# fp32 weight pieces on the SyncE queue, and a few transposes moved between DMA and TensorE, in a fused BigBird attention and gMLP kernel

## The chip, the cores and the metric

The kernel runs on one core of one Trainium2 chip. The metric is the time of one execution in device microseconds, as the median of several runs. Beside the runs there is one profiled execution. Its span goes from the first to the last instruction of the program; its own time is a little longer than the span.

## The reference

What is computed is block-sparse attention followed by a gMLP layer with a spatial gate:

```python
scores = scale * np.matmul(q, k.transpose(0, 1, 3, 2))       # (4, 8, 768, 768), scale = 1/8
# mask: blocks of 32; neighbours, first and last block, 3 sampled blocks per block
scores = np.where(mask, scores, -1000000000.0)
attn = softmax(scores)                                       # with 1e-09 in the sum
x = np.matmul(attn, v)                                       # to (4, 768, 8 * 64)

h = np.maximum(x @ w_in, 0.0)                                # w_in (512, 1024)
u, v = h[..., :512], h[..., 512:]
v_n = (v - mean(v)) / np.sqrt(var(v) + 1e-06)
v_s = np.einsum('ts,bsd->btd', w_spatial, v_n) + b_spatial[None, :, None]   # w_spatial (768, 768)
out = (u * v_s) @ w_out                                      # w_out (512, 512), fp32 out
```

All inputs but the sampled blocks are fp32. The batch is 4, with 8 heads of 64 and a sequence of 768.

## The kernel before

The work is cut into 16 pairs of heads (4 pairs to a batch), and each pair into 12 slots, so that the main loop is an order written out by hand: for each slot of each pair it issues the scores of one 128-row chunk of keys, one exp of 128x768 on ScalarE (line 260), the product with v of the chunk seven slots back (`av`, line 272), and whatever else is hung on that slot. Every engine runs its own instructions in this program order. The tile framework inserts the waits on semaphores.

The life of a pair p is this. `load` (line 95) brings q, k, v as fp32 on the SyncE queue, three pairs ahead, in slot 7 of pair p-3 (pairs 0 to 2 at the start). The staging tiles `st_q`, `st_k`, `st_v` have two buffers each. `prepare` (lines 109 and 112) casts them on Pool in slot 7 of pair p-2, k first, then q, then v; v goes to one of three `vv` buffers. Then q and k have to be transposed. For pairs 1 to 4 this is done on TensorE in thirds (`tr_pair`, lines 206 and 211: two transposes in each of six slots, then copies from PSUM by VectorE), in slots 4 to 9 of pair p-1 (6 to 11 for pair 1). For later pairs it is done by a DMA transpose on the SyncE queue (`tr_dma`, line 239) in slot 10 of pair p-2, and VectorE copies the halves in slots 5 and 9 of pair p-1 (`split_pair`, line 245).

After the last `av` of a head VectorE normalises it (`norm`, lines 285 and 286), in slots 0 and 6. The normalised pair is transposed to `xt` in slot 8 of the next pair (`xtr`): by a DMA transpose on the SyncE queue (line 299), or, for the last pair of a batch, by six transposes on TensorE and one copy (lines 295 and 297).

The gMLP of batch 0 begins after slot 8 of pair 4. Its 24 units (six each of v, u, spatial and out; lines 348, 371, 393, 411) are spread over the 48 slots that follow by a budget of TensorE time. The same happens for batches 1 and 2; the last batch is run at the end, alone. The gMLP's buffers `un`, `vsb`, `vn`, `gn`, `gt` have two copies each of 6 KB per partition and stand empty until pair 4.

The weights come by three DMAs on Pool's queue, which cast fp32 to bf16 on the way: w_spatial in slot 0 of pair 0 (line 463), w_in and w_out in slot 7 of pairs 0 and 1 (lines 470 and 473). w_spatial is transposed on TensorE, 36 blocks with six copies, in slots 0 to 3, 10 and 11 of pairs 2 and 3 (`wspt_third`, lines 312 and 317).

Three things about waits matter below. A load waits until the cast on Pool has freed its buffer. The SyncE queue issues in program order[...]. PSUM has two buffers for scores, two for `av` and two (`moe`) for transposes and gMLP units.

Of the kernel before, what the change touches and what calls it, by code (L numbers as in the profile page):

```python
# [10 lines left out]
FP32 = mybir.dt.float32  # L11
BF16 = mybir.dt.bfloat16
# [14 lines left out]
def kernel(  # L27
# [16 lines left out]
    nc = tc.nc  # L44

    B, H, S, D = q.shape
# [3 lines left out]
    NCH = S // 128  # L50
# [3 lines left out]
    DH = DFF // 2  # L54
    NDM = DM // 128
    NDH = DH // 128
    NG = H // 2
    NP = B * NG
# [5 lines left out]
    work = ctx.enter_context(tc.tile_pool(name="work", bufs=1))  # L64
    psum = ctx.enter_context(tc.tile_pool(name="psum", bufs=1, space=bass.MemoryType.PSUM))
    ctx.enter_context(tc.manual_schedule())

    ident = const.tile([128, 128], BF16)
    warm = const.tile([128, 512], BF16)
    w_in_t = const.tile([128, NDM, DFF], BF16)  # L70
    w_out_t = const.tile([128, NDH, DM], BF16)
    ws_nat = const.tile([128, NCH, S], BF16)
    w_spt = const.tile([128, NCH, S], BF16)
# [10 lines left out]
    def dram(src, b, h0, nh):  # L84
        return src[b, h0:h0 + nh].rearrange("h (p c) d -> p h (c d)", c=NCH)

    def st_tile(p, nm):
        st[nm, p] = work.tile([128, 2, NCH * D], FP32, tag=f"st_{nm}", bufs=2, name=f"st_{nm}")
        return st[nm, p]

    def load(p, names="qkv", eng=nc.sync):
        b, g = divmod(p, NG)
        for nm, src in (("q", q), ("k", k), ("v", v)):
            if nm in names:
                eng.dma_start(out=st_tile(p, nm), in_=dram(src, b, 2 * g, 2))
# [3 lines left out]
    def nat_tile(p, nm):  # L99
        nat[nm, p] = work.tile([128, NCH, 2, D], BF16, tag=f"nat_{nm}", bufs=2,  # L100
                               name=f"nat_{nm}")

    def cast_qk(p, nm, hs, eng):
        src = st[nm, p][:, hs].rearrange("p h (c d) -> p h c d", d=D)
        dst = nat[nm, p].rearrange("p c h d -> p h c d")[:, hs]
        if eng is nc.scalar:
            nc.scalar.activation(out=dst, in_=src, func=AF.Copy)
        else:
            eng.tensor_copy(out=dst, in_=src)  # L109

    def cast_v(p):
        nc.gpsimd.tensor_copy(  # L112
            out=vv[p % 3][:, :, :, 0:D],
            in_=st.pop(("v", p)).rearrange("p h (c d) -> p h c d", d=D))

    def prepare(p):
        for nm in "kq":
            nat_tile(p, nm)
            cast_qk(p, nm, slice(0, 2), nc.gpsimd)
        cast_v(p)  # L120

    samp_i = const.tile([NB, 2 * NR], I32)
    stq, stk = st_tile(0, "q"), st_tile(0, "k")
# [21 lines left out]
    def keep_warm(n, cols):  # L145
        for _ in range(n):
            nc.tensor.matmul(out=wps[:, 0:cols], lhsT=warm[:, 0:128], rhs=warm[:, 0:cols],  # L147
                             start=True, stop=True)
# [50 lines left out]
    tr_ps = {}  # L199
# [30 lines left out]
    def second_head():  # L230
        mask_rows(1)
        cast_qk(0, "k", slice(1, 2), nc.vector)
        cast_qk(0, "q", slice(1, 2), nc.vector)
# [15 lines left out]
    a_ref, av_ref, xn_ref, xt_ref = {}, {}, {}, {}  # L249

    def qk_exp(j, ci):
        if ci == 0:
            a_ref[j] = work.tile([128, NCH, S], BF16, tag="a_all", bufs=3, name="a_all")
        ps = psum.tile([128, 1024], FP32, tag="sc", bufs=2)
        for hf in range(2):
            nc.tensor.matmul(out=ps[:, hf * 512:hf * 512 + HALF],  # L256
                             lhsT=kt[j % 4][:, ci * 128:(ci + 1) * 128],
                             rhs=qt[j % 4][:, hf * HALF:(hf + 1) * HALF],
                             start=True, stop=True)
        nc.scalar.activation(  # L260
            out=a_ref[j][:, ci, :].rearrange("p (b c) -> p b c", b=2),
            in_=ps.rearrange("p (b c) -> p b c", b=2)[:, :, 0:HALF],
            func=AF.Exp, scale=0.125)
# [15 lines left out]
    def norm(j):  # L279
        p, h = divmod(j, 2)  # L280
        if h == 0:
# [4 lines left out]
        nc.vector.tensor_tensor(out=xn_ref[p][:, :, h, :], in0=ps[:, :, 0:D],  # L286
                                in1=rc.to_broadcast([128, NCH, D]), op=ALU.mult)

    def xtr(p):
        xn = xn_ref.pop(p)  # L290
        xt_ref[p] = work.tile([128, S], BF16, tag="xt", bufs=8, name="xt")
        if p % NG == NG - 1:
            ps = psum.tile([128, S], BF16, tag="moe", bufs=2)
            for c in range(NCH):
                nc.tensor.transpose(out=ps[:, c * 128:(c + 1) * 128], in_=xn[:, c],
                                    identity=ident)
            nc.vector.tensor_copy(out=xt_ref[p], in_=ps)
        else:
            nc.sync.dma_start_transpose(
                out=xt_ref[p].rearrange("p (c n) -> p c n", c=NCH),  # L300
                in_=xn.rearrange("p c h d -> p (c h d)"))


    ws_ps = {}

    def wspt_third(i):
        sc, third = divmod(i, 3)
        if third == 0:
            ws_ps[0] = psum.tile([128, S], BF16, tag="moe", bufs=2, name="ps_ws")
        ps = ws_ps[0]  # L310
        for tcc in (2 * third, 2 * third + 1):
            nc.tensor.transpose(
                out=ps[:, tcc * 128:(tcc + 1) * 128],
                in_=ws_nat[:, tcc, :].rearrange("p (s c) -> p c s", c=NCH)[:, sc, :],
                identity=ident)
        if third == 2:
            nc.vector.tensor_copy(out=w_spt[:, sc, :], in_=ps)

    tail_tags = deque(["sc", "av", "moe"])

# [109 lines left out]
    for p in range(NP + 1):  # L430
        for s in range(12):
            g = 12 * p + s
            j, ci = divmod(g, NCH)
            if p == NP and g - LAG >= 2 * NP * NCH:
                break
            if p < NP:
                qk_exp(j, ci)
            if p == 0 and s == 0:
                second_head()
            if p == 0 and s < 6:  # L440
                keep_warm(2, 128)
            if p == 0 and s == 3:
                tr_head(1, "k", dve_copy)
            if p == 0 and s == 4:
                tr_head(1, "q", dve_copy)
                mask_rows(2)
                mask_rows(3)
            if p + 1 <= NG:
                first = 4 if p else 6
                if first <= s < first + 3:  # L450
                    tr_pair(p + 1, "k", s - first)
                elif first + 3 <= s < first + 6:
                    tr_pair(p + 1, "q", s - first - 3)
            elif p + 1 < NP and s in (5, 9):
                split_pair(p + 1, "k" if s == 5 else "q")
            if s == 10 and NG < p + 2 < NP:
                tr_dma(p + 2, "k")
                tr_dma(p + 2, "q")
            if p == 0 and s == 0:
                cast_v(0)  # L460
                prepare(1)
                load(2)
                nc.gpsimd.dma_start(out=ws_nat,
                                    in_=moe_w_spatial.rearrange("(p c) s -> p c s", c=NCH))
            if s == 7 and p + 2 < NP:
                if p + 3 < NP:
                    load(p + 3)
                prepare(p + 2)
                if p == 0:
                    nc.gpsimd.dma_start(out=w_in_t,  # L470
                                        in_=moe_w_in.rearrange("(g p) f -> p g f", p=128))
                if p == 1:
                    nc.gpsimd.dma_start(out=w_out_t,
                                        in_=moe_w_out.rearrange("(g p) f -> p g f", p=128))
            if moe_q and slots_left > 0:
                budget += sum(u[0] for u in moe_q) / slots_left
                slots_left -= 1
                while moe_q and budget >= moe_q[0][0] / 2:
                    ns, run = moe_q.popleft()
                    run()  # L480
                    budget -= ns
            if g >= LAG:
                ja, qc = divmod(g - LAG, NCH)
                av(ja, qc)
                if qc == NCH - 1:
                    norm(ja)
            if p in (2, 3) and not 4 <= s < 10:
                for i in range(3 * (s if s < 4 else s - 6) // 2, 3 * (s + 1 if s < 4 else s - 5) // 2):
                    wspt_third(9 * (p - 2) + i)
            if s == 8 and p >= 1:  # L490
                xtr(p - 1)
                if p % NG == 0:
                    moe_q.extend(moe_units(p // NG - 1))
                    slots_left = 48
                    budget = 0.0
# [35 lines left out]
```

## Time and profile before

| what | value |
|---|---|
| median of 7 runs | 232.79 us (231.63 to 235.83) |
| profiled execution, its own time | 233.34 us |
| its span | 231.6 us |
| TensorE matmul busy | 216.5 us, 93% of the span |
| ScalarE busy | 171.3 us, 74% |
| VectorE busy | 132.2 us, 57% |
| Pool busy | 51.5 us, 22% |
| DMA moved | 37.32 MB, mean 161 GB/s |
| mean granted TensorE clock | 0.985 |

Busy time is the union of the instructions of an engine. Matmuls are pipelined and their ends are modelled, so that a TensorE shown as busy is not at its peak. PEld is the loading of weights into TensorE's array and overlaps the matmuls. The DMA figure counts written bytes. A wait is put down to the instruction or transfer that ended it last.

### The profile page before, as it was taken

How to read it: one execution, taken by the hardware profiler on the slowest of the kernel's cores; microseconds unless marked ns; L12 is line 12 of the kernel's file. 1: busy time of each engine (PE TensorE's matmuls, PEld its weight loads, DVE VectorE, ACT ScalarE, POOL GpSimd, SP SyncE). 2: the span in 40 equal slices, each digit the busy share in tenths (PEclk: the TensorE clock that was granted, in tenths of full speed). 3: DMA queues.
4: the chain of work that ended last, by engine and by line, in shares of the span. 5: the costliest groups of instructions: out<-in, count | busy, mean ns of one | idle time of the engine just before them, and what ended most of it. 6: DMA issues, size and time to landing. Idle time of an engine off the chain costs nothing.

```text
span 231.6 us, 5286 instructions
## 1 busy us (share of the span) xinstructions
PE 216.5 (93%) x2125; PEld 131.9 (57%) x2154; DVE 132.2 (57%) x285; ACT 171.3 (74%) x245; POOL 51.5 (22%) x82
## 2 busy tenths in 40 slices
PE   7899999939999999999999999999999999999993
PEld 3567787625556555566566555666565555544551
DVE  6683575315799334347996444359992333576432
ACT  5899999943689866796799667887799676257241
POOL 5332650440126401020153401210160000012000
PEclk9999999995999999999999999999999999999999
DMA  6579999999309584799928372999240323520015
GB/s 214 194 222 215 367 182 180 330 225 331 105 0 108 201 116 81 231 228 301 336 44 200 109 136 49 268 284 282 43 96 9 76 52 63 198 94 0 0 48 228
DMA packets 54941, 37.32 MB, mean 161 GB/s; under 512 B 38404, under 2 KB 51204, under 8 KB 54788
## 3 DMA queue, kind: packets, MB, share of 16 engines
q1 hardware_dynamic: 53428, 33.83, 57.3%
q0 software_dynamic: 1200, 2.75, 7.0%
q8 instruction: 17, 0.28, 0.5%
q10 hardware_dynamic: 288, 0.39, 0.5%
q14 instruction: 8, 0.07, 0.1%
HBM read 24.38 MB, written 6.29 MB: 132 GB/s over the span
## 4 chain that ended last, share of the span: by engine, by line
PE 81%; DMA 6%; ACT 6%; DVE 2%; issue 2%; SPq 1%; POOL 0%; POOLq 0%
PE ps L256 25%; PE ps_av L272 12%; PE ps_moe L393 10%; PE ps_moe L348 7%; PE ps_moe L371 7%; ACT a_all L260 6%; PE ps_moe L411 6%; DMA st_k<-in_k_dram 5%; PE ps_t L393 2%; PE wps L147 2%; PE ps_t L348 2%; PE ps_t L411 1%; PE ps_t L371 1%; PE ps_sc L393 1%; DMA out_dram<-osb 1%
## 5 line engine op out<-in xcount | busy, mean ns | idle before, releaser
L260 ACT ACTIVATE a_all<-ps 128x768 bf16<-128x768 f32 x192 | 143.2, 811 | 36.8 <-PE ps L256 36.5
L256 PE MATMUL ps<-qt,kt 88*128 88x384 bf16 x384 | 94.6, 327 | 4.4 <-ACT a_all L260 3.2
L272 PEld LDWEIGHTS <-a_all 128*128 128x128 bf16 x1152 | 61.0, 98 | 30.0 <-issue 1.2
L272 PE MATMUL ps_av<-vv,a_all 128*128 128x65 bf16 x1152 | 68.0, 194 | 0.0
L256 PEld LDWEIGHTS <-kt 88*128 88x128 bf16 x384 | 28.9, 98 | 8.2 <-issue 5.2
L396 DVE SCALAR_TENSOR_TENSOR gn<-ps_moe,b_col,un 128x512 bf16<-128x512 f32 x18 | 13.5, 751 | 28.2 <-PE ps_moe L393 28.2
L393 PE MATMUL ps_moe<-vn,w_spt 128*128 128x512 bf16 x99 | 24.8, 378 | 0.5
L112 POOL CAST vv<-st_v 128x768 bf16<-128x768 f32 x16 | 13.6, 851 | 47.6 <-PE ps_av L272 39.3
L393 PEld LDWEIGHTS <-w_spt 128*128 128x128 bf16 x144 | 13.8, 97 | 14.3
L348 PE MATMUL ps_moe<-w_in_t,xt 128*128 128x512 bf16 x66 | 19.5, 401 | 0.5 <-DMA st_k<-in_k_dram 0.2
L109 POOL CAST nat_k<-st_k 128x768 bf16<-128x768 f32 x15 | 12.5, 835 | 32.4 <-DMA st_k<-in_k_dram 20.9
L361 POOL TENSOR_SCALAR std<-mv 128x3 f32<-128x3 f32 x8 | 1.9, 243 | 78.0 <-DVE mv L358 65.8
L286 DVE TENSOR_TENSOR xn<-ps_av,rc 128x384 bf16<-128x384 f32 x32 | 17.8, 558 | 1.4 <-DVE rc L285 0.3
L411 PE MATMUL ps_moe<-w_out_t,gt 128*128 128x512 bf16 x66 | 18.1, 378 | 0.3
L371 PE MATMUL ps_moe<-w_in_t,xt 128*128 128x512 bf16 x66 | 17.7, 378 | 0.3
L357 DVE BATCH_NORM_STATS2 stats<-vsb 128x6 f32<-128x512 bf16 x24 | 16.7, 695 | 1.9 <-ACT vsb L352 1.3
L348 PEld LDWEIGHTS <-xt 128*128 128x128 bf16 x96 | 9.7, 101 | 11.0 <-issue 2.2
L371 PEld LDWEIGHTS <-xt 128*128 128x128 bf16 x96 | 9.3, 97 | 9.5
L418 DVE COPY osb<-ps_moe 128x512 f32<-128x512 f32 x9 | 6.2, 692 | 14.9 <-PE ps_moe L411 14.8
L354 DVE TENSOR_SCALAR vsb<-ps_moe 128x512 bf16<-128x512 f32 x18 | 12.3, 682 | 3.4 <-PE ps_moe L348 3.4
L411 PEld LDWEIGHTS <-gt 128*128 128x128 bf16 x96 | 8.9, 97 | 8.4
L375 DVE TENSOR_SCALAR vn<-vsb,mv,rstd 128x512 bf16<-128x512 bf16 x24 | 12.7, 566 | 0.6 <-POOL rstd L363 0.5
(85 smaller groups left out, 181.7 us busy)
## 6 DMA issues: line engine op xcount, KB each, us to landing
st_v<-in_v_dram SPq DMA_DIRECT2D x16, 384.0 KB, 5.8
out_dram<-osb SPq DMA_DIRECT2D x24, 256.0 KB, 2.6
st_q<-in_q_dram SPq DMA_DIRECT2D x15, 384.0 KB, 4.3
st_k<-in_k_dram SPq DMA_DIRECT2D x15, 384.0 KB, 5.0
ws_nat<-in_moe_w_spatial_dram POOLq DMA_DIRECT2D x1, 1152.0 KB, 11.5
w_in_t<-in_moe_w_in_dram POOLq DMA_DIRECT2D x1, 1024.0 KB, 13.3
w_out_t<-in_moe_w_out_dram POOLq DMA_DIRECT2D x1, 512.0 KB, 13.1
st_k<-in_k_dram ACTq DMA_DIRECT2D x2, 192.0 KB, 2.9
```

The costliest lines, as they stand in the source:

```text
L112: nc.gpsimd.tensor_copy(out=vv[p % 3][:, :, :, 0:D], in_=st.pop(("v", p)).rearrange("p h (c d) -> p h c d", d=D))
L256: nc.tensor.matmul(out=ps[:, hf * 512:hf * 512 + HALF], lhsT=kt[j % 4][:, ci * 128:(ci + 1) * 128], rhs=qt[j % 4][:, hf * HALF:(hf + 1) * ...
L260: nc.scalar.activation(out=a_ref[j][:, ci, :].rearrange("p (b c) -> p b c", b=2), in_=ps.rearrange("p (b c) -> p b c", b=2)[:, :, 0:HALF], ...
L272: nc.tensor.matmul(out=av_ref[j][:, qc, :], lhsT=a_ref[j][:, ci, qc * 128:(qc + 1) * 128], rhs=vv[p % 3][:, h, ci, :], start=(ci == 0), st ...
L286: nc.vector.tensor_tensor(out=xn_ref[p][:, :, h, :], in0=ps[:, :, 0:D], in1=rc.to_broadcast([128, NCH, D]), op=ALU.mult)
L348: nc.tensor.matmul(out=ps, lhsT=xt(g)[:, tcc * 128:(tcc + 1) * 128], rhs=w_in_t[:, g, DH:DFF], start=(g == 0), stop=(g == NDM - 1))
L357: nc.vector.bn_stats(out=stats, in_=vsb[:, tcc, :])
L371: nc.tensor.matmul(out=ps, lhsT=xt(g)[:, tcc * 128:(tcc + 1) * 128], rhs=w_in_t[:, g, 0:DH], start=(g == 0), stop=(g == NDM - 1))
L375: nc.vector.tensor_scalar(out=vn[:, tcc, :], in0=vsb[:, tcc, :], scalar1=mv[:, tcc, 0:1], scalar2=rstd[:, tcc:tcc + 1], op0=ALU.subtract, ...
L393: nc.tensor.matmul(out=ps, lhsT=w_spt[:, sc, tcc * 128:(tcc + 1) * 128], rhs=vn[:, sc, :], start=(sc == 0), stop=(sc == NCH - 1))
L396: nc.vector.scalar_tensor_tensor(out=gn[:, tcc, :], in0=ps, scalar=b_col[:, tcc:tcc + 1], in1=un[:, tcc, :], op0=ALU.add, op1=ALU.mult)
L411: nc.tensor.matmul(out=ps, lhsT=gt[:, tcc, dhc, :], rhs=w_out_t[:, dhc, :], start=(dhc == 0), stop=(dhc == NDH - 1))
```

## The change

The three casting DMAs on Pool's queue are removed. In their place nine pieces are loaded as fp32 by the SyncE queue into tiles that take the buffers `un`, `vsb`, `vn`, `gn`, `gt` of the gMLP in turn: four pieces of w_in (0.5 MB each), three of w_spatial (0.8 MB each) and two of w_out (0.5 MB each). They are loaded two at pair 0 slot 0, two at pair 0 slot 7, two at pair 2 slot 7 and one at pair 3 slot 7 (w_spatial), and two at pair 5 slot 7 (w_out), each time after q, k, v that are loaded in that slot. Pool casts two pieces each in slot 7 of pairs 0, 1 and 6, after `prepare`. VectorE casts the three pieces of w_spatial in slots 4 and 11 of pair 3 and 4 of pair 4, and its writes reorder the columns.

The transposes of w_spatial move from TensorE to six DMA transposes on the SyncE queue, two each at pair 3 slot 11, pair 4 slot 5 and pair 5 slot 1. The x of pairs 0 to 2 is transposed on TensorE in thirds, in slots 8 to 10 of pairs 1 to 3, in place of three DMA transposes. The q and k of pair 5 are transposed on TensorE as well, in place of two DMA transposes. The transposes of q and k by TensorE for pairs 2 to 4 move from slots 4 to 9 to slots 0 to 5, where those of pair 5 stand too.

```diff
+    w_pieces = deque()
+    for g in range(NDM):
+        w_pieces.append((moe_w_in.rearrange("(g p) f -> p g f", p=128)[:, g:g + 1],
+                         w_in_t[:, g:g + 1, :]))
+    for c2 in range(3):
+        w_pieces.append((moe_w_spatial.rearrange("(p c) s -> p c s", c=NCH)[:, 2 * c2:2 * c2 + 2],
+                         ws_nat[:, 2 * c2:2 * c2 + 2, :].rearrange(
+                             "p t (c s) -> p t s c", c=NCH)))
+    for g in range(NDH // 2):
+        w_pieces.append((moe_w_out.rearrange("(g p) f -> p g f", p=128)[:, 2 * g:2 * g + 2],
+                         w_out_t[:, 2 * g:2 * g + 2, :]))
+    w_staged = deque()
+    w_tags = deque(["un", "vsb", "vn", "gn", "gt"])
+
+    def load_weights(n):
+        for _ in range(n):
+            src, dst = w_pieces.popleft()
+            a, f = src.shape[1:]
+            t = work.tile([128, NCH * DH // 2], FP32, tag=w_tags[0], bufs=2,
+                          name="wst")[:, 0:a * f].rearrange("p (a f) -> p a f", a=a)
+            w_tags.rotate(-1)
+            nc.sync.dma_start(out=t, in_=src)
+            if len(dst.shape) == 4:
+                t = t.rearrange("p a (s c) -> p a s c", c=NCH)
+            w_staged.append((t, dst))
+
+    def cast_weights(n, eng=nc.gpsimd):
+        for _ in range(n):
+            t, dst = w_staged.popleft()
+            eng.tensor_copy(out=dst, in_=t)
...
+    def xtr_third(p, third):
+        if third == 0:
+            xt_ref[p] = work.tile([128, S], BF16, tag="xt", bufs=8, name="xt")
+            tr_ps["x"] = psum.tile([128, S], BF16, tag="moe", bufs=2, name="ps_x")
+        ps = tr_ps["x"]
+        for c in (2 * third, 2 * third + 1):
+            nc.tensor.transpose(out=ps[:, c * 128:(c + 1) * 128], in_=xn_ref[p][:, c],
+                                identity=ident)
+        if third == 2:
+            xn_ref.pop(p)
+            nc.vector.tensor_copy(out=xt_ref[p], in_=ps)
...
-    def wspt_third(i):
...
+    def wspt(tcc):
+        nc.sync.dma_start_transpose(out=w_spt[:, :, tcc * 128:(tcc + 1) * 128],
+                                    in_=ws_nat[:, tcc, :])
...
-            if p + 1 <= NG:
-                first = 4 if p else 6
+            if p <= NG:
+                first = 0 if p else 6
...
-            if s == 10 and NG < p + 2 < NP:
+            if s == 10 and NG + 1 < p + 2 < NP:
                 tr_dma(p + 2, "k")
                 tr_dma(p + 2, "q")
             if p == 0 and s == 0:
                 cast_v(0)
                 prepare(1)
                 load(2)
-                nc.gpsimd.dma_start(out=ws_nat,
-                                    in_=moe_w_spatial.rearrange("(p c) s -> p c s", c=NCH))
+                load_weights(2)
             if s == 7 and p + 2 < NP:
                 if p + 3 < NP:
                     load(p + 3)
+                if p in (0, 2, 3, 5):
+                    load_weights((2, 0, 2, 1, 0, 2)[p])
                 prepare(p + 2)
-                if p == 0:
-                    nc.gpsimd.dma_start(out=w_in_t,
-                                        in_=moe_w_in.rearrange("(g p) f -> p g f", p=128))
-                if p == 1:
-                    nc.gpsimd.dma_start(out=w_out_t,
-                                        in_=moe_w_out.rearrange("(g p) f -> p g f", p=128))
+                if p in (0, 1, 6):
+                    cast_weights(2)
...
-            if p in (2, 3) and not 4 <= s < 10:
-                for i in range(3 * (s if s < 4 else s - 6) // 2, 3 * (s + 1 if s < 4 else s - 5) // 2):
-                    wspt_third(9 * (p - 2) + i)
-            if s == 8 and p >= 1:
+            if (p, s) in ((3, 4), (3, 11), (4, 4)):
+                cast_weights(1, nc.vector)
+            if (p, s) in ((3, 11), (4, 5), (5, 1)):
+                tcc = 2 * ((3, 11), (4, 5), (5, 1)).index((p, s))
+                wspt(tcc)
+                wspt(tcc + 1)
+            if 1 <= p < NG and 8 <= s < 11:
+                xtr_third(p - 1, s - 8)
+            if s == 8 and p >= NG:
                 xtr(p - 1)
```

More of the change, by code (lines that the diff above doesn't have):

```diff
@@ L287, in norm @@
                                 in1=rc.to_broadcast([128, NCH, D]), op=ALU.mult)
+    def xtr_third(p, third):
[9 more added lines that the diff above has]
+            nc.vector.tensor_copy(out=xt_ref[p], in_=ps)
     def xtr(p):
-        xn = xn_ref.pop(p)
-        xt_ref[p] = work.tile([128, S], BF16, tag="xt", bufs=8, name="xt")
         if p % NG == NG - 1:
[L293 to L297, printed above, removed]
-        else:
+            for third in range(3):
+                xtr_third(p, third)
+        else:
+            xn = xn_ref.pop(p)
+            xt_ref[p] = work.tile([128, S], BF16, tag="xt", bufs=8, name="xt")
             nc.sync.dma_start_transpose(
@@ L301, in xtr @@
                 in_=xn.rearrange("p c h d -> p (c h d)"))
-    ws_ps = {}
-    def wspt_third(i):
[L307 to L317, printed above, removed]
+    def wspt(tcc):
+        nc.sync.dma_start_transpose(out=w_spt[:, :, tcc * 128:(tcc + 1) * 128],
+                                    in_=ws_nat[:, tcc, :])
     tail_tags = deque(["sc", "av", "moe"])
```

## The prediction

> **What bounds the kernel now.** I read the page's 40 slices of 5.79 us first, to see which engine is full in which part of the run.
>
> ```profile
> PE   7899999939999999999999999999999999999993
> ...
> ACT  5899999943689866796799667887799676257241
> ...
> PEclk9999999995999999999999999999999999999999
> DMA  6579999999309584799928372999240323520015
> ```
>
> ScalarE is full up to about 46 us (attention alone: one exp per slot), TensorE from about 58 us on (gMLP units mixed in). Between them lie a dip of both engines, the only slice with a lower clock (52 to 58 us), and the DMA engines full since about 17 us. The table of stretches, cut at the starts of exps 12, 24, 36, 48, 60 and 72 (counted from 0 along ScalarE's timeline; a pair has 12, one per slot), puts a size on it. Columns: length, then busy time (and instructions) of PE, PEld, DVE, ACT, POOL, then clock, DMA share and GB/s.
>
> ```profile
> 16.69:25.20 8.51, 8.23 (x114) 6.06 (x111) 3.73 (x8) 8.51 (x12) 2.53 (x4) 1.00 1.01 254
> 25.20:33.80 8.60, 8.60 (x130) 6.86 (x128) 5.23 (x11) 8.60 (x14) 6.11 (x8) 1.00 1.09 258
> 33.80:42.70 8.90, 8.90 (x131) 7.04 (x129) 5.66 (x13) 8.61 (x13) 0.00 (x0) 1.00 1.21 234
> 42.70:59.56 16.86, 12.15 (x110) 7.39 (x110) 5.28 (x13) 8.90 (x12) 4.76 (x6) 0.80 1.15 290
> 59.56:71.11 11.55, 11.44 (x118) 6.91 (x117) 11.06 (x25) 9.87 (x14) 3.97 (x7) 1.00 0.09 18
> ```
>
> Pairs 1 to 3 take 8.5 to 8.9 us with ScalarE busy throughout: their rate is one exp per 0.70 us. Pair 4 takes 16.86 us at a mean clock of 0.80. Why, the waits and the timeline tell (start, length, engine, line, operation, count, idle time before it and what ended that):
>
> ```profile
> POOL nat_k L109 <- DMA st_k<-in_k_dram: 20.9, 5, 9.8
> DVE kt L245 <- DMA tt_k<-nat_k: 8.5, 3, 7.3
> PE ps L295 <- DVE xn L286: 3.9, 1, 3.9
> ```
>
> ```profile
> 50.91 0.72 DVE L245 COPY kt<-tt_k 64x768 bf16<-64x768 bf16 x2 [7.30 <-DMA tt_k<-nat_k]
> ...
> 51.77 0.56 DVE L286 TENSOR_TENSOR xn<-ps_av,rc 128x384 bf16<-128x384 f32 x1
> ...
> 52.38 0.82 PE L295 MATMUL ps<-ident,xn 128*128 128x128 bf16 x6 [3.88 <-DVE xn L286]
> ...
> 53.63 0.63 PE L348 MATMUL ps_moe<-w_in_t,xt 128*128 128x512 bf16 x1
> ...
> 53.88 0.81 ACT L260 ACTIVATE a_all<-ps 128x768 bf16<-128x768 f32 x1 [4.71 <-PE ps L256]
> ```
>
> VectorE, in order, stood 7.30 us for k of pair 5, transposed by DMA. Behind that copy stood the norm of pair 3, behind the norm its transposes on TensorE (3.88 us idle), behind those the exps (4.71 us). TensorE then ran at half clock: 0.63 us for a 512-column matmul that takes 0.378 us later. The SyncE queue shows why k of pair 5 came late:
>
> ```profile
> 28.52 0.89 SPq L95 DMA_DIRECT2D st_k<-in_k_dram  x1
> 29.51 2.10 SPq L95 DMA_DIRECT2D st_v<-in_v_dram  x1
> 31.66 7.93 SPq L299 DMA_TRANSPOSE xt<-xn  x1
> ...
> 44.38 3.25 SPq L239 DMA_TRANSPOSE tt_k<-nat_k  x1
> ```
>
> Its load, issued at 28.52, landed 14.6 us later, since the transfers of the casting weight loads (11.5, 13.3 and 13.1 us to land) and the transposes of x (14.4 and 13.2 us) shared the engines with it. The transpose was issued at 44.38 and took 6.5 us more.
>
> [...] q, k, v of pair 1, almost alone, landed at 9.4, 10.4, 11.4 us, one 393 KB tensor per 1.0 us; beside the casting load, v of pair 2 took 11.2 us. [...] the 128x384 fp32 cast took 356 ns, the 64x768 bf16 copy out of PSUM 555 ns, so 384 elements more cost 199 ns, 0.52 ns each, over 157 ns fixed. For scattered writes no row here shows it.
>
> **The stall, priced.** From exp 56 to exp 57 before: 48.35 to 53.88, 5.53 us. Without the wait TensorE has in that slot the scores (0.33), values (0.27) and six transposes (0.4): 1.0 us. Gain 4.5. Exp 57 to 60 took 5.68 us at half clock; the same slots of the next batch (exps 105 to 108) took 3.44. Gain 2.2. From there on the first batch runs as the second does: exps 60 to 96 and 108 to 144 both take 37.37 us. **6.7 us can be had, if no wait takes its place.**
>
> **The change, part by part.**
>
> Transposes: five DMA transposes (x of pairs 0 to 2, k and q of pair 5) leave the stretch before 48 us; one alone fills the engines for about 1.0 us (0.2 MB at some 200 GB/s where transposes run alone, 130 to 150 us), so 5 us of DMA and their queue time (7.93 us of SyncE in one of them) go. Six come back for w_spt, issued after exp 47 and up to the start of pair 5. TensorE loses 36 transposes (w_spt) and gains 12 + 18: six fewer, spread two per slot where ScalarE limits: nothing. VectorE loses six copies of 558 ns and gains three of x (550) and three casts of 1536 elements, 157 + 1536 x 0.52 = 0.96 us each (1.8 if the scattered write falls to half rate). It was busy 5.7 of 8.9 us, so as busy time: nothing.
>
> Weights: three software issues on Pool go (0.8 us each), six casts of 1024 come, 1.1 us each by the 830 ns of 768: 6.6 us on an engine with 22% busy: nothing. The DMA reads the same 5.5 MB. Before, the engines moved some 258 GB/s of written bytes from 13.5 to 42 us, 7.4 MB, of which 2.75 MB were casts read at double size: 10.1 MB in 28.5 us, 356 GB/s at the source. The new order on SyncE from 12.08 us is pair 2, w_in 0 and 1, pair 3, w_in 2 and 3, pair 4, pair 5, ws 0 and 1, pair 6, ws 2. At 393 GB/s, first landing 15.5 us as before: k2 16.5, w_in 1 at 20.2, k3 22.2, k4 27.9, k5 31, ws 0 at 34, ws 2 at 41.
>
> New waits. (a) TensorE's transposes of pair p+1 move from slots 4 to 9 up to slots 0 to 5. For pair 2 that is exp 12, where TensorE is free at about 16.5; nat_k of pair 2 is ready at 16.5 + 0.83 = 17.4. Behind stand the values of that slot and the scores of exp 13: exp 13 starts near 18.4 instead of 17.39, **loss 1.05 us**. Bounds: 0 (k lands a microsecond sooner) to 2.4 (as late as before, nat_k ready at 18.8). Pairs 3, 4, 5 are needed at 26, 34.7, 43 and ready at 23, 29, 32: nothing, covered by 3 us or more. (b) VectorE's casts of ws 0, 1, 2 are in slots 40, 47, 52 (about 37.5, 42.5, 46): landed by then, 3.5 us to spare for ws 0. The cast in slot 52 shares VectorE with q copies (1.1) and the norm of pair 3 (0.75) ahead of TensorE's transposes in slot 56: 46.2 + 0.96 + 1.1 + 0.75 = 49.0 against 49.4, free at full rate, 0.6 late at half. I take **0.3**, ends 0 and 0.9. (c) SyncE waits for the casts before issuing w_spt; behind it are loads of pair 7 and the transposes of pair 6, needed at about exp 65: over 5 us to spare. (d) w_spt is needed in pair 6, w_out in pair 7: hidden.
>
> Sum: 6.7 - 1.05 - 0.3 = **5.4 us**. The profiled execution took 233.34 (span 231.6), so 227.9 with span 226.2. Its time is 0.55 above the median of seven, so against the median, 232.79: **227.4**.
>
> **Rivals.** *Larger new waits in pair 1 and 4, otherwise the same:* k of pair 2 as late as before (2.4) and the casts at half rate (0.9): 3.4 us gained, **229.4**; with a further microsecond of Pool or VectorE lateness 230.4. For it: Pool waited 4.27 us for that very load in the profile; against: the casting load beside it is gone.
>
> *Slower: VectorE stands in slot 40 for ws 0.* That piece is the last of 7.6 MB counted from pair 2. Behind the cast stand the q copies and the norm of pair 2's second head, needed by TensorE's x transposes in slot 44 (41 us); the norm is ready 2.85 us after the landing. Lost is landing + 2.85 - 41, so the 5.4 us are used up at a landing of 43.6, and it is clearly slower from 44.3, a rate below 247 GB/s from 13.5 us on. At 235 GB/s it lands at 45.8: 7.7 us lost, **235.1**. For it: 254 to 258 GB/s moved in those stretches before, so little is missing. Against: that rate counts written bytes of casts and small transpose packets; at 356 the piece lands by 35.
>
> *No change:* the stall only moves, to ws 2 at slot 52 or to pair 6 in pair 5, because the queue is as full as before; the landing is then near 43.5 and the sum zero, **232.8**. Against it: the engines are at 0.00 from 60 to 69 us, so the last transposes have room.
>
> **How the numbers follow.** Main case 0.66, 227.4 (226.1 to 228.7 by the bounds of (a) and (b)); larger waits 0.19; no change 0.05; slower 0.10. A measurement of this kernel tells about 0.3% (0.7 us) from no change. So faster 0.85, same 0.05, slower 0.10. The range, 225.9 to 230.8, holds the first two cases and leaves out the others.
>
> **What would show it.** Right: exps 48 to 60 in about 10.4 us (5.65 + 1.0 + 0.3 + 3.44) instead of 16.86; clock 1.00 in every slice after the start; no long idle of VectorE before a transposed tile; 0.5 to 1.5 us of TensorE or ScalarE idle at exp 12 or 13, released by Pool's nat_k; loads landing in 4 to 9 us. Wrong: VectorE idle before its ws casts, ScalarE gaps at exps 24, 36 or 44, or a gain that is taken back after exp 60.

## The result, and the profile after

The changed kernel takes 239.01 us (median of 12 runs, 237.78 to 240.07). The kernel before took 232.79. The ratio is 1.030, with a 95% interval of 1.027 to 1.033: **slower by 3.0%, where 227.4 us and a gain of 2.3% had been forecast.** The profiled execution took 240.05 us with a span of 238.3.

First the slices of the page (5.96 us each now):

```profile
PE   8999999592999999999999999999999999999993
...
ACT  5699999392478976788779866796899766346341
...
PEclk9999999798599999999999999999999999999999
DMA  6599997319971948399965565699522223430015
```

Where there was one dip of TensorE there are two, at 42 to 48 us and at 54 to 60 us; the clock is lower in both and for 6 us after the second. The DMA row, which was full there before, falls to 3 and 1 from 42 us on. The stretches are cut as before, at the starts of exps 12, 24, 36, 48, 60 and 72 (length; busy PE, PEld, DVE, ACT, POOL; clock, DMA share, GB/s):

```profile
18.58:27.09 8.51, 8.40 (x121) 6.32 (x119) 4.28 (x9) 8.51 (x12) 6.45 (x8) 1.00 1.05 393
27.09:35.60 8.51, 8.40 (x120) 6.33 (x117) 4.28 (x9) 8.51 (x13) 4.70 (x6) 1.00 1.04 392
35.60:48.67 13.07, 10.10 (x123) 7.37 (x120) 9.65 (x11) 8.90 (x13) 4.45 (x3) 0.87 0.50 158
48.67:66.18 17.51, 12.30 (x120) 7.94 (x120) 12.84 (x15) 8.90 (x12) 4.61 (x1) 0.81 0.77 186
66.18:77.73 11.55, 11.44 (x118) 6.90 (x117) 11.06 (x25) 9.86 (x14) 3.95 (x7) 1.00 0.43 134
```

Pairs 1 and 2 run as fast as ScalarE allows, and the loads at 393 GB/s. Pair 3 takes 13.07 us instead of 8.90, pair 4 17.51 instead of 16.86. What is new in the two is VectorE: 9.65 and 12.84 us busy, against 5.66 and 5.28. Its timeline from 38 us on, with the first instruction on TensorE and ScalarE that waits for it:

```profile
38.15 4.11 DVE L153 CAST ws_nat<-wst 128x1536 bf16<-128x1536 f32 x1
...
42.28 1.12 DVE L244 COPY qt<-ps_tr 64x768 bf16<-64x768 bf16 x2
43.43 0.20 DVE L318 RECIPROCAL rc<-ps_av 128x6 f32<-128x6 f32 x1
43.66 0.56 DVE L319 TENSOR_TENSOR xn<-ps_av,rc 128x384 bf16<-128x384 f32 x1
44.28 0.29 PE L328 MATMUL ps_x<-ident,xn 128*128 128x128 bf16 x2 [2.88 <-DVE xn L319]
...
45.03 0.81 ACT L293 ACTIVATE a_all<-ps 128x768 bf16<-128x768 f32 x1 [2.96 <-PE ps L289]
...
47.24 4.15 DVE L153 CAST ws_nat<-wst 128x1536 bf16<-128x1536 f32 x1
...
52.95 4.07 DVE L153 CAST ws_nat<-wst 128x1536 bf16<-128x1536 f32 x1
57.05 1.12 DVE L244 COPY qt<-ps_tr 64x768 bf16<-64x768 bf16 x2
...
58.43 0.56 DVE L319 TENSOR_TENSOR xn<-ps_av,rc 128x384 bf16<-128x384 f32 x1
59.05 0.82 PE L328 MATMUL ps_x<-ident,xn 128*128 128x128 bf16 x6 [4.58 <-DVE xn L319]
...
60.55 0.81 ACT L293 ACTIVATE a_all<-ps 128x768 bf16<-128x768 f32 x1 [5.41 <-PE ps L289]
```

The casts of w_spatial take 4.1 us each, where the forecast had 0.96 and at most 1.8. They wait for no transfer: no idle time is shown in front of them. Behind the first stand, in VectorE's order, the q copies, the norm of pair 2, TensorE's transposes of x, and the exps. Behind the third stands the same chain for pair 3, and it ends in the same place as the old stall: TensorE idle for 4.58 us instead of 3.88, then a clock of 0.50 (60 to 63 us; before, 53 to 57 us). The second cast has a part in that: from 46.76 to 59.0 us VectorE works without a pause, so the second pushes the third. The chain of waits from 36 to 62 us says the same by shares:

```profile
by line: DVE ws_nat L153 46.5%; PE ps L289 9.8%; DVE qt L244 8.5%; DVE kt L244 8.2%; DVE xn L319 6.5%; PE ps_x L328 6.0%; PE ps_moe L379 5.7%; PE ps_av L305 3.3%; issue 2.3%; DVE xt L332 2.1%; DVE rc L318 1.7%; PE ps_tr L239 0.9%
```

The difference of the two spans, 6.7 us, splits up along the starts of the exps. Exp 0 starts 1.74 us later (8.89 against 7.15). Exps 0 to 44 take the same time (32.37 and 32.33). Exps 44 to 48 take 7.41 instead of 3.22, **4.2 more**. Exp 56 to 57 takes 6.23 instead of 5.53, **0.7 more**. From exp 57 on nothing differs by over 0.1 us. The late start comes ahead of everything that the change touches. TensorE is slower there: six transposes of q at 6.54 us take 0.85 us, against 0.52 at 5.45 before. One of the kernels below, whose program is the same up to slot 40 of the main loop (the scattered casts on Pool), has 0.52 in its profile and starts exp 0 at 7.51. In the others exp 0 starts at 7.3 to 8.9 us, and 8.90 belongs to one of the quickest. So the late start is not taken as an effect of the change; why TensorE's pace differs there stays open.

### The profile page after: what moved, and what is told of

Read it like the earlier page. It is cut to its first block, busy times and chain, and to the rows that moved or that the text cites. A ratio compares the mean times of both kernels' runs of the same rounds, so it can differ in the third digit from the quotient of the medians.

```text
span 238.3 us, 5284 instructions
## 1 busy us (share of the span) xinstructions
PE 220.3 (92%) x2119; PEld 133.8 (56%) x2148; DVE 143.1 (60%) x285; ACT 171.7 (72%) x245; POOL 61.3 (26%) x85
## 4 chain that ended last, share of the span: by engine, by line
PE 78%; ACT 10%; DVE 9%; issue 1%
PE ps L289 22%; PE ps_av L305 11%; ACT a_all L293 10%; PE ps_moe L424 10%; PE ps_moe L379 7%; PE ps_moe L442 6%; PE ps_moe L402 6%; DVE ws_nat L153 5%; PE wps L180 2%; PE ps_t L424 2%; PE ps_t L379 2%; PE ps_t L442 1%; PE ps_t L402 1%; DVE qt L244 1%; PE ps_sc L424 1%
## 5 line engine op out<-in xcount | busy, mean ns | idle before, releaser
L289 PE MATMUL ps<-qt,kt 88*128 88x384 bf16 x384 | 96.8, 334 | 3.5 <-ACT a_all L293 2.5
L112 POOL CAST vv<-st_v 128x768 bf16<-128x768 f32 x16 | 19.3, 1206 | 56.9 <-PE ps_av L305 52.2
L289 PEld LDWEIGHTS <-kt 88*128 88x128 bf16 x384 | 29.4, 99 | 7.1 <-issue 4.6
L318 DVE RECIPROCAL rc<-ps_av 128x6 f32<-128x6 f32 x32 | 6.3, 196 | 12.2 <-PE ps_av L305 12.1
```

Of the source, the lines that this page charges most:

```text
L112: nc.gpsimd.tensor_copy(out=vv[p % 3][:, :, :, 0:D], in_=st.pop(("v", p)).rearrange("p h (c d) -> p h c d", d=D))
L289: nc.tensor.matmul(out=ps[:, hf * 512:hf * 512 + HALF], lhsT=kt[j % 4][:, ci * 128:(ci + 1) * 128], rhs=qt[j % 4][:, hf * HALF:(hf + 1) * ...
```

## The experiments

The theory after this reading (A): the step that failed is the price of one instruction. A cast on VectorE whose successive writes lie far apart costs four times what was reckoned (4.1 us, not 0.96), and stands in order ahead of a norm. Rivals: casts on VectorE and Pool slow each other, and the 4.1 us come from that (B); any cast of that size is slow or any cast at that place does harm (C); late loads (D). The ratios below are to runs of the kernel before that were made beside each group of kernels: 233.01 us for the plain cast, the scatter on the read side and the scattered casts on Pool, 232.40 for the other four. These kernels ran 4 to 6 times each, the scattered casts on Pool 19 times, the transposes alone 22 times.

**The price alone.** A kernel of nothing but casts of 1536 elements: written densely; with the changed kernel's scattered write; read 24 bytes apart and written densely; and written 4, 8, 16 and 32 bytes apart. First VectorE alone, then Pool alone (without the last four), then both.

```diff
+    def scatter(eng, s, d):
+        eng.tensor_copy(out=d.rearrange("p (t c s) -> p t s c", t=2, c=NCH),
+                        in_=s.rearrange("p (t s c) -> p t s c", t=2, c=NCH))
+    def gather(eng, s, d):
+        eng.tensor_copy(out=d.rearrange("p (t c s) -> p t c s", t=2, c=NCH),
+                        in_=s.rearrange("p (t s c) -> p t c s", t=2, c=NCH))
+    def step(eng, s, d, n):
+        eng.tensor_copy(out=d.rearrange("p (t a n) -> p t n a", t=2, n=n),
+                        in_=s.rearrange("p (t n a) -> p t n a", t=2, n=n))
```

> A kernel of nothing but casts of 1536 fp32 elements to bf16 (it computes none of the reference; its own time means nothing). Theory A, the scattered write: on VectorE, alone, the plain cast takes about 0.96 us, the scattered write (256 bytes between successive elements) about 4.1 us with no Pool work beside it, a gathered read (24 bytes apart) with a dense write below 1.8 us[...]. Theory B[...]: alone the scattered write is as quick as the plain one, and 4 us appears only where Pool casts run beside it. Theory C, any cast of this size or shape is slow: plain, scattered and gathered all take about 4 us.

One instruction of each kind from this kernel's timeline, in that order, VectorE first:

```profile
8.87 0.96 DVE L76 CAST o<-a 128x1536 bf16<-128x1536 f32 x1 [7.48 <-DMA a<-in_moe_w_spatial_dram]
11.86 4.01 DVE L79 CAST o<-a 128x1536 bf16<-128x1536 f32 x1
24.00 1.52 DVE L83 CAST o<-a 128x1536 bf16<-128x1536 f32 x1
28.65 1.02 DVE L87 CAST o<-a 128x1536 bf16<-128x1536 f32 x1
30.76 1.88 DVE L87 CAST o<-a 128x1536 bf16<-128x1536 f32 x1
34.58 3.57 DVE L87 CAST o<-a 128x1536 bf16<-128x1536 f32 x1
41.78 3.47 DVE L87 CAST o<-a 128x1536 bf16<-128x1536 f32 x1
...
49.48 1.46 POOL L76 CAST o<-b 128x1536 bf16<-128x1536 f32 x1 [49.03 <-DVE b L104]
54.06 7.02 POOL L79 CAST o<-b 128x1536 bf16<-128x1536 f32 x1
75.30 2.86 POOL L83 CAST o<-b 128x1536 bf16<-128x1536 f32 x1
89.39 4.46 POOL L91 CAST o<-b 128x768 bf16<-128x768 f32 x1
```

The plain cast is the forecast's 0.96 us to the digit. The scattered write takes 4.01 with Pool idle: B falls, and so does the part of C that says that any such cast is slow. The four lines of L87 are writes 4, 8, 16 and 32 bytes apart: 1.02, 1.88, 3.57, 3.47 us. So most of the cost is there at 16 bytes (3.57, against 4.01 at 256 bytes), and at 8 bytes the time is already doubled (1.88, against 0.96). A scattered read, 24 bytes apart, costs far less, 1.52. Pool pays too: 1.46, 7.02, 2.86. The last line is a cast of 768 elements on Pool beside scattered casts on VectorE: 4.46 us for what takes 0.83 in the attention kernels. In the changed kernel two casts of v on Pool took 2.91 and 4.61 us and ended 0.7 us after the cast of w_spatial beside them; that looks like the same thing, and nobody waited for them.

So the price is measured, and its mechanism is not shown. Distance alone does not set it: reads 24 bytes apart took 1.52 us, writes 16 bytes apart 3.57. Why a cast on Pool takes 4.46 us beside scattered casts on VectorE, no run shows either.

**The cast made plain.** The reordering of the columns is left out, nothing else; w_spatial is then applied with its columns permuted.

```diff
-                         ws_nat[:, 2 * c2:2 * c2 + 2, :].rearrange(
-                             "p t (c s) -> p t s c", c=NCH)))
+                         ws_nat[:, 2 * c2:2 * c2 + 2, :]))
...
-            if len(dst.shape) == 4:
-                t = t.rearrange("p a (s c) -> p a s c", c=NCH)
```

> The changed kernel with the three casts of w_spatial writing densely, in natural order: the reordering of its columns is left out, so w_spatial is applied with permuted columns. Theory A (the price of the scattered write is what failed): each cast takes 0.96 to 1.1 us, exps 44 to 48 take some 2.9 us instead of 7.4, exp 56 to 57 about 1.0 to 1.3 instead of 6.2, the clock stays at 1.00, and the time is 239.0 - 4.4 - 5.1 - 2.2 = 227.3 us, faster than the kernel before by 2.0 to 2.5%. Theory C (any cast at these places holds the norm up, whatever it takes): 236 us or more. Rival D (the stall at pair 4 comes from late loads): 232 to 234 us, VectorE idle before its casts.

227.6 us, 0.976 of the kernel before (0.968 to 0.983). The same stretches of this kernel for pairs 3 and 4, and its first cast:

```profile
35.62:44.43 8.81, 8.70 (x123) 6.55 (x120) 6.06 (x12) 8.58 (x14) 2.37 (x3) 1.00 0.91 227
44.43:54.27 9.84, 9.45 (x120) 6.70 (x120) 7.23 (x14) 8.79 (x12) 0.83 (x1) 1.00 0.83 202
```

```profile
38.16 0.95 DVE L150 CAST ws_nat<-wst 128x1536 bf16<-128x1536 f32 x1
```

Pair 4 takes 9.84 us instead of 17.51 (16.86 before), at full clock. Both stalls are gone with 3.15 us taken off each of three instructions that keep their place, so the place alone does no harm (the rest of C), and the loads were in time (D).

**The scatter moved to the read side.** The result stays that of the changed kernel.

```diff
-                             "p t (c s) -> p t s c", c=NCH)))
+                             "p t (c s) -> p t c s", c=NCH)))
...
-                t = t.rearrange("p a (s c) -> p a s c", c=NCH)
+                t = t.rearrange("p a (s c) -> p a c s", c=NCH)
```

> The changed kernel with the same result, but the three casts of w_spatial read 24 bytes apart and write densely instead of the reverse. Theory A1 (only the write side is dear): casts of 1.0 to 1.8 us and a time of 227 to 229 us. Theory A2 (distance between successive elements costs on either side): casts of 3 to 4.1 us and 234 to 239 us.

228.25 us, 0.980 (0.974 to 0.986): A1. Casts of 1.56 us leave small delays of the two norms:

```profile
38.15 1.57 DVE L153 CAST ws_nat<-wst 128x1536 bf16<-128x1536 f32 x1
...
41.75 0.29 PE L328 MATMUL ps_x<-ident,xn 128*128 128x128 bf16 x2 [0.34 <-DVE xn L319]
...
50.99 0.51 PE L328 MATMUL ps_x<-ident,xn 128*128 128x128 bf16 x6 [0.33 <-DVE xn L319]
```

TensorE's wait for the norms goes from none to 0.3 to 2.9 and 4.6 us, as the cast goes from 0.95 to 1.56 to 4.1.

**The scattered casts on Pool.**

```diff
-                cast_weights(1, nc.vector)
+                cast_weights(1)
```

> The changed kernel with the three casts of w_spatial on Pool instead of VectorE, at the same places, still with the scattered write. Theory A: VectorE is free, the norms of pairs 2 and 3 come in time, and the time is 227 to 229 us even if Pool takes 4 us or more for each cast, since nothing urgent stands behind them on Pool. Theory B[...]: Pool's casts hold up VectorE's copies too, and the time stays above 233 us.

234.79 us, 1.008 (1.005 to 1.010), a miss of the expectation. The norms come in time (exp 44 to 48 in 3.17 us, exp 56 to 57 in 0.84), but exp 48 is 1.0 us late, and most is lost later: exps 60 to 96 take 44.6 us instead of 37.4.

```profile
43.77 0.28 PE L239 MATMUL ps_tr<-ident,nat_k 128*128 128x128 bf16 x2 [1.29 <-POOL nat_k L109]
```

```profile
45.21 13.90 POOL L153 CAST ws_nat<-wst 128x1536 bf16<-128x1536 f32 x2
58.71 1.05 POOL L109 CAST nat_k<-st_k 128x768 bf16<-128x768 f32 x1
```

```profile
59.78 1.23 SPq L272 DMA_TRANSPOSE tt_k<-nat_k  x1
```

```profile
62.72 0.72 DVE L278 COPY kt<-tt_k 64x768 bf16<-64x768 bf16 x2 [4.10 <-DMA tt_k<-nat_k]
```

```profile
64.09 1.02 PE L402 MATMUL ps_moe<-w_in_t,xt 128*128 128x512 bf16 x3 [2.82 <-DVE vsb L385]
```

7.0 us a piece was too much for Pool as well. The cast of k of pair 5 stands behind the first of them on Pool, and TensorE waited 1.29 us for it. The cast of k of pair 6 stands behind the other two; its DMA transpose was issued at 59.78, as soon as the cast had ended. VectorE waited 4.10 us for it, with the relu of a gMLP unit behind that, and TensorE stood 2.82 us. At 77.63 VectorE waited once more, 5.25 us, for k of pair 7; that wait was not taken apart. "Nothing urgent stands behind them on Pool" was wrong: the casts of k do. That is the dear cast in front of urgent work once more (theory A with another engine), and not B.

**The gathered casts behind a norm.** Two at pair 3 slot 6, one at pair 4 slot 0.

```diff
-            if (p, s) in ((3, 4), (3, 11), (4, 4)):
-                cast_weights(1, nc.vector)
+            if (p, s) in ((3, 6), (4, 0)):
+                cast_weights(2 if p == 3 else 1, nc.vector)
```

> The gathered-read kernel (228.25 us) with its three casts of w_spatial moved on VectorE from slots 4 and 11 of pair 3 and 4 of pair 4 to directly behind a norm: two at pair 3 slot 6, one at pair 4 slot 0. Theory A with place (what costs is only that part of a cast that delays a norm which TensorE's transposes of x wait for): the stalls left at exp 44 (1.14 us for one exp) and 56 (1.35) shrink to 0.7 to 0.9, and the time is 227.0 to 227.7 us. Rival (what is left is the busy time of VectorE, wherever it is): no change, 228.2.

227.7 us, 0.981 (0.977 to 0.985). In the profile exp 44 to 45 fell from 1.14 to 0.70 us, exp 56 to 57 only from 1.35 to 1.20. The interval overlaps that of the kernel it comes from, so the time does not decide between the two expectations.

**The gathered casts on Pool.** The edit of the scattered Pool version, on the gathered kernel.

> The gathered-read kernel with its three casts on Pool at the same places (2.9 us each there by the price kernel, against 7.0 for the scattered write). Theory A: VectorE has nothing of them, Pool stays ahead of the statistics of the first gMLP batch, and the time is 227.0 to 227.8 us. Rival (work on Pool delays casts of pairs 6, 7 or the statistics, as in the scattered Pool version, 234.8): 229 us or more, with TensorE idle near exps 68 and 79.

227.57 us, 0.981 (0.977 to 0.985), as expected by A: at 2.9 us each no exp comes late, and exps 0 to 191 take 181.5 us, the least of all (188.7 before, 193.6 with the change).

**The weights alone.** The gathered kernel with x of pairs 0 to 2 and q, k of pair 5 transposed by DMA again, and q, k of pairs 2 to 4 back in slots 4 to 9.

```diff
-            if p <= NG:
-                first = 0 if p else 6
+            if p + 1 <= NG:
+                first = 4 if p else 6
...
-            if 1 <= p < NG and 8 <= s < 11:
-                xtr_third(p - 1, s - 8)
-            if s == 8 and p >= NG:
+            if s == 8 and p >= 1:
                 xtr(p - 1)
```

> One part alone: weights as fp32 pieces, gathered casts on VectorE and w_spatial transposed by DMA as in the changed kernel, but x of pairs 0 to 2 and q, k of pair 5 transposed by DMA in their old slots, and q, k of pairs 2 to 4 in slots 4 to 9. Theory E (the old stall came from the order of the DMA queue, which the pieces mend): 228 to 230 us, exps 56 to 57 below 2 us. Theory F (the DMA transposes themselves, in front of a late k of pair 5, made the stall): the wait of VectorE for the transposed k of pair 5 stays at 3 us or more and the time is 231 to 234 us.

227.95 us, 0.983 (0.979 to 0.987). Pair 4, cut at its exps 48 and 60:

```profile
42.80:52.64 9.84, 9.29 (x111) 6.14 (x110) 7.64 (x15) 8.79 (x12) 2.54 (x3) 1.00 0.98 141
```

```profile
46.50 0.72 DVE L278 COPY kt<-tt_k 64x768 bf16<-64x768 bf16 x2 [0.58 <-DMA tt_k<-nat_k]
```

The old stall is gone with five DMA transposes still in place. VectorE waited 0.58 us for the transposed k of pair 5 instead of 7.30: theory E. The loads of pair 5 come much sooner: its q landed at 30.9 us, against 42.1 before. At 227.95 us this part alone is as quick as the whole change with gathered casts (228.25), so with the pieces in place the moved transposes gained nothing that these runs show.

**The transposes alone.** The kernel before with x of pairs 0 to 2 and q, k of pair 5 on TensorE and the early slots; weights and w_spatial as before.

> The other part alone: the kernel before with x of pairs 0 to 2 and q, k of pair 5 on TensorE and the early slots, but the casting weight DMAs and the transposes of w_spatial on TensorE as before. Theory F: no wait for a transposed tile at pair 4 is left, so 6.7 us are gained there; back go some 2 us at exp 12, where k of pair 2 is late beside the casting load, and 1 to 2.5 us in pairs 2 and 3, where TensorE has up to five transposes in a slot: 228.5 to 231 us. Theory E: loads beside casting DMAs land so late that TensorE waits for casts of pairs 3 to 5 instead, and the time stays at 232 us or more.

231.6 us, 0.996 (0.994 to 0.999), between the two expectations. Pairs 2, 3 and 4:

```profile
25.36:36.27 10.91, 9.49 (x139) 7.30 (x140) 5.68 (x12) 9.04 (x13) 4.62 (x6) 1.00 1.12 257
36.27:46.59 10.32, 9.68 (x141) 7.33 (x138) 6.10 (x14) 9.04 (x12) 4.80 (x6) 1.00 1.12 317
46.59:56.44 9.85, 9.44 (x121) 6.62 (x119) 6.37 (x13) 8.80 (x13) 0.83 (x1) 1.00 0.55 151
```

The old stall is gone here as well: pair 4 takes 9.85 us. So either part takes it away by itself, and F and E were no alternatives. What goes back is in pairs 2 and 3, 10.91 and 10.32 us where the kernel before took 8.60 and 8.90: 3.7 us, more than the 1 to 2.5 expected. Up to six transposes stand in a slot there, and TensorE waits 0.89 us for k of pair 3. At exp 12, where 2 us had been expected, nothing was lost. The dense kernel, which has the same early transposes but not the 36 of w_spatial, took 8.51 and 8.81 us for these pairs. So the DMA transposes of w_spatial most likely pay by taking 36 transposes out of these slots; they were not tested by themselves.

## Why the prediction was wrong, point by point

- **What bounds the kernel, and what can be had: right.** The stall at pair 4 was put at 6.7 us. With dense casts pair 4 takes 9.84 instead of 16.86 us, 7.0 less, at full clock. The low clock, counted in that sum with 2.2 us, came again in the changed kernel: 4.58 us idle, then 0.50 from 60 to 63 us and a 512-column matmul in 0.63 us.
- **The loads: right.** 393 GB/s had been assumed and 393 and 392 were measured; k of pair 3 landed at 23.1 us (22.2 forecast), the first piece of w_spatial at 34.9 (34).
- **(a), the early transposes: mis-sized.** 1.05 us had been set for exp 12; it cost nothing in any kernel (exp 12 to 13 takes 0.71 us in all). k of pair 2 landed at 15.1 us, not 16.5, and its cast was done at 16.0, while TensorE came to it only after 18. The load was issued at 11.4 us, against 12.5 before. That is not owed to the new weight loads: the kernel with the transposes alone, which has the old ones, issued it at 10.9. The bound of 0 covered it.
- **(b), the casts of w_spatial: this is the step that failed.** The text took 0.96 us each and "1.8 if the scattered write falls to half rate". Measured: 4.1. The lower value was the author's estimate from two rows with dense writes (the price kernel took 0.96), the upper one from an assumed half rate, and no row bounded what a scattered write costs. It was noted that no row showed scattered writes, yet a bound was written down as if one did. With 4.1 in its place, and from the start that the profile shows, its own addition for pair 4 gives 52.95 + 4.07 + 1.1 + 0.75 = 58.9 us for the norm, which came at 59.0. The same addition at slot 44 gives 38.15 + 4.11 + 1.1 + 0.75 = 44.1 against 44.2. One thing it did not add up is the row of casts: the second pushed the third, which began 4.3 us after exp 48, against 2.5 with dense casts. So none of the 6.7 us is left, and 4.2 + 0.7 come on top: 232.8 + 4.9 = 237.7 us, out of the measured 239.0. The other 1.3 us stay open; the late start of the profile, 1.74 us, is of that size.
- **"As busy time: nothing": wrong in kind.** VectorE had room on average. What counted was what stood behind the cast in its queue.
- **The slower rival: right place, wrong cause.** The text has the chain by name, VectorE in slot 40, then the q copies, the norm and the x transposes in slot 44, and sets 0.10 on it. It looked for the delay in the landing of the piece and did not ask what happens if the cast itself is long. In (b) slot 52 alone was priced, and not slot 40, where 4.2 us were lost.
- **(c), (d): right.** The loads of pair 7 were issued at 54.1, and no exp after 57 lost time.
- **Three small slips in its sums,** none of which bears on the failure. 18.4 less 17.39 is a loss of 1.0 us, not 1.05. A cast at half rate puts the norm at 46.2 + 1.8 + 1.1 + 0.75 = 49.85, 0.45 us late, not 0.6. And 228.7 takes in the upper bound of (a) alone; with that of (b) it is 229.4, the rival that follows.

The forecast of 227.4 us is what the change gives once that one instruction writes densely: 227.6 without the reordering, 227.6 to 228.3 with it. That the figures agree so closely is partly luck. In the dense kernel none of the 1.05 us of (a) was lost, and exps 0 to 191 gained 7.0 us; but in its profile, as in that of the changed kernel, exp 0 starts at 8.90 us, 1.75 later than before, which no term foresaw.

## What to carry to other kernels

Before an instruction is moved to a busy in-order engine, price it in its own access pattern: the cast took 0.96 us with dense writes and 3.57, 3.47 and 4.01 with neighbouring elements written 16, 32 and 256 bytes apart. If no row of the profile shows such an instruction, its upper bound is open until a small kernel has timed it. If a reordering has to be done somewhere, try it with the reads apart and the writes dense: at 24 bytes that cost 1.52 us here; other distances of reads were not measured. Then ask what stands behind it in the queue, not how busy the engine is: 0.95, 1.56 and 4.1 us in the same place were worth 227.6, 228.3 and 239.0 us.

## What the runs showed of the hardware that was not expected

- VectorE, 1536 fp32 elements to bf16: 0.96 us dense; written 4, 8, 16, 32 and 256 bytes apart 1.02, 1.88, 3.57, 3.47 and 4.01 us; read 24 bytes apart 1.52 us.
- Pool, the same cast: 1.46 us dense, 7.02 written 256 bytes apart, 2.86 read 24 bytes apart.
- A cast of 768 elements on Pool, 0.83 us in the attention kernels, took 4.46 us beside a row of scattered casts on VectorE; the last of those took 4.52 instead of 4.01.
- The clock of TensorE fell after it had been idle for 2.88 us (slot 44 of the changed kernel: 0.50 from 45 to 48 us, 0.87 over pair 3), 3.88 us (kernel before: 0.50 from 53 to 57 us) and 4.58 us (slot 56 of the changed kernel: 0.50 from 60 to 63 us), but not after 2.82 us (scattered casts on Pool: 1.00 from 53.8 to 68.4 us).
